# Moving conversions, an expansion and the block products of a sketched-attention + GELU-MLP kernel to other steps

## The chip, the cores and the metric

The kernel runs on one core of one Trainium2 chip. The metric is the device time of one execution in microseconds (us). Before the change it is 276.03 us, the median of three runs (275.75 to 277.18). The profiled execution, on which all readings of the trace rest, has a span of 274.7 us.

A core has a matrix engine (TensorE, "PE" in the profile), a vector engine (VectorE, "DVE"), an engine for activation functions (ScalarE, "ACT"), a general one (GpSimd, "POOL") and queues that issue transfers. They run at the same time, each through its own list of instructions in a fixed order, and wait for one another by semaphores.

## The reference, cut to what matters

Four batches of four heads with 1088 tokens each go through an attention without softmax: queries and keys are expanded to 64 features (the outer product of two 8-vectors), and since no softmax lies between them the keys and values are first reduced to one 64x32 matrix per head. The result feeds an MLP with an exact GELU.

```python
def phi(x):                                     # 32 -> 64 features
    a = einsum('rd,bhsd->bhsr', S1, x); b = einsum('rd,bhsd->bhsr', S2, x)
    return einsum('bhsi,bhsj->bhsij', a, b).reshape(..., 64)
q_p, k_p = phi(q), phi(k)
kv  = einsum('bhsf,bhsd->bhfd', k_p, v)         # one 64x32 matrix per head
z   = sum(k_p, axis=2)
num = einsum('bhsf,bhfd->bhsd', q_p, kv)
den = einsum('bhsf,bhf->bhs', q_p, z)[..., None] + 1e-06
x   = (num / den), heads joined to 128 columns  # 4352 x 128
h   = x @ w_in                                  # 4352 x 2048
out = (0.5 * h * (1 + erf(h / sqrt(2)))) @ w_out   # 4352 x 128
```

The weights `w_in`, `w_out` and the sketches arrive as 64-bit floats, so the kernel converts them to 32 bits itself.

## The kernel before

The 4352 tokens are cut into nine chunks: eight of 512 tokens (two for each batch) and a last one with the remainders. The hidden layer is cut into 16 tiles of 128 channels. One **step** `t` is one hidden tile of one chunk: a matmul of 128x128 weights on 512 tokens, and a GELU. Chunks 0 and 1 share steps 0 to 31; chunk `n` from 2 on has steps 16n to 16n+15. In each step everything else that is due is put into the text, and the text's order is the order of every engine.

```python
steps  = [(n, fi) for f in range(0, USUAL, 4) for n in range(NCH) for fi in range(f, f + 4)]   # 0..15
steps += [(n, fi) for n in range(NCHUNK) for fi in range(USUAL if n < NCH else 0, NF)]          # 16..143
# [...]
for t in range(len(steps) + LAG):
    # [...] (steps 0 to 4 have pieces of their own)
    for n in drains[t]:
        drain(n)
    if t < len(steps):
        n, fi = steps[t]
        hidden(n, fi, by_halves=t >= 18 and (n < NMAIN or fi < 5))
    if [... last tile of a block of four ...]:
        token_sums(n, b)
    for f in slots[t]:          # what at(t, f) has put there
        f()
    for n in done[t]:
        store(n)
    if t != 4:
        for f, *a in products[t]:
            f(*a)
```

**Second product.** Tiles 0 to 7 of chunks 0 and 1 go through a plain matmul (`project`). All others go through a Strassen-like scheme in blocks of four tiles: GpSimd forms sums of the block's halves, TensorE does seven pairs of half-size products, and two PSUM banks hold a chunk's sums until they are drained. `out_bank()` takes one of only **two** banks of the pool `ops`, so a chunk's first product waits until all reads of the bank's former content are over.

```python
ops = ctx.enter_context(tc.tile_pool(name="ops", bufs=2, space=PSUM))
wps = ctx.enter_context(tc.tile_pool(name="wps", bufs=2, space=PSUM))   # two tiles of two banks

def token_sums(n, b):                      # 4 GpSimd operations of 128x512
    pool.tensor_sub(out=s[3], in0=a11, in1=a21)     # L606, tile bits_low
    pool.tensor_add(out=s[1], in0=a21, in1=a22)     # L607, bits_a
    pool.tensor_sub(out=s[2], in0=s[1], in1=a11)    # L608, bits_e
    pool.tensor_sub(out=s[4], in0=a12, in1=s[2])    # L609, bits_m

def two_products(n, b, i):
    # [...]
    if opens and i == 0:
        acc[n] = [out_bank(), out_bank()]
    for name, e in zip(two[:2], two[2:]):
        pe.matmul(acc[n][bank][...], lhsT=fixed, rhs=moving, ...)      # L641

def drain(n):
    C, N = (att.tile([128, 2, CW], FP, name="sums") for i in range(2))
    a0, a1 = acc[n]
    act.copy(out=C[lo, 0], in_=a1[hi])                                    # L653
    act.copy(out=N[hi, 0, one], in_=a1[hi, one])                          # L654
    act.copy(out=N[lo, 0, one], in_=a0[lo, one])                          # L655
    dve.tensor_add(out=C[lo, 1], in0=a1[lo], in1=C[lo, 0])                # L657
    for half in (lo, hi):
        dve.tensor_add(out=C[half, 0, one], in0=a0[lo, one], in1=C[lo, 1, two])    # L659
    dve.tensor_add(out=C[hi, 0, two], in0=a0[hi, two], in1=C[hi, 0, one])  # L660
    dve.tensor_add(out=N[hi, 1, one], in0=a0[hi, one], in1=C[hi, 0, two])  # L661
    dve.tensor_add(out=N[lo, 1, one], in0=a0[lo, two], in1=N[lo, 0, one])  # L662
```

**Attention of a chunk, and the next batch's keys** (n = 3 stands at step 37):

```python
def query_turn(n):   dve.transpose(out=qT[n], in_=q_sb[n])             # L453
def query_expand(n):                                                    # 4 matmuls, 4 copies, 4 products
    expand_products(n)                    # L462, into two tiles of wps
    for g in range(4):
        expand_copy(n, g)                 # ACT L469
        if g % 2: expand_multiply(n, g // 2)     # DVE L483

def attend(n, meanwhile):
    banks = halves(work_banks())
    # 4 matmuls, L504
    meanwhile()                           # features_of_all(b): key products L350, ACT copies L817
    for h in range(H):
        act.activation(out=den[h * D:(h + 1) * D, :W], ..., func=ACT.Copy, bias=1e-6)     # L511
    dve.reciprocal(out=den[:, :W], in_=den[:, :W])                        # L512
    for h in range(H):
        dve.tensor_mul(out=xT[n][rows, :W], in0=banks[h % 2][rows, :W], in1=den[rows, :W])   # L516

def outer_of_all(b):
    for r, a in enumerate(held["factors"]):
        for t in range(2):
            dve.tensor_mul(...)           # L827, k_p from a_t and PSUM
    for r in range(2):
        add_tokens(b, r, dve)             # L388 and L391, from SBUF to SBUF
```

**Keys of batch 1** (steps 14 to 21) come in smaller pieces: `key_turn_blocks` (DVE L335), `features` (PE L350, ACT L366, DVE L367, each in a tile of `wps` of its own), `add_tokens` by GpSimd, `turn_keys_rem` (PE L306 into the next tile of `wps`), `features_rem`, `finish_keys` (PE L396, L425), `turn_kv`.

**Conversion of a weight piece** of 512 columns (class `Rounding`): `low_words` (ACT L250), `fields` (DVE L254, L256), `exponents` (ACT L262), and `finish`, which is `mantissas` (DVE L270), `signs` (DVE L275) and `product` (L280, by VectorE unless another engine is named). `channel_sums(i)` is four GpSimd operations on a converted piece of `w_out` (L593 to L596).

The schedule that the change touches:

```python
def round_at(t, w):
    r = []
    at(t, lambda: (r.append(Rounding(w)), r[0].low_words(), r[0].fields()))
    at(t + 1, lambda: (r[0].exponents(), r[0].finish()))

for i, (t0, t1) in enumerate(((4, 6), (8, 10), (12, 17))):
    round_at(t0, w_in_sb[i + 2]); round_at(t1, w_out_sb[i + 2])
for i, t in enumerate((25, 26, 28, 13, 19)):
    at(t, channel_sums, i)
# keys of batch 1, with t = 32: widen_v_rem 12, key_turn_blocks 14, features and add_tokens 15,
# turn_keys_rem 16, features_rem 17, query_turn(2) 18, finish_keys 19, turn_kv 21,
# query_expand(2) 22, query_turn(3) 23, attend(2) 25
for n in range(3, NCHUNK):
    t = (n - 1) * NF
    # [...]
    if n > 3: at(t - 2, query_turn, n)
    at(t + 2 if n > 3 else t - 2, query_expand, n)
    at(t + 5, attend, n, lambda b=b, keys=keys: keys and features_of_all(b))
    if keys:
        at(t + 5, outer_of_all, b)        # n = 3: step 37
```

Of the kernel before, what the change touches and what calls it, by code (L numbers as in the profile page):

```python
# [16 lines left out]
def kernel(  # L17
# [18 lines left out]
    pe, dve, act, pool, sp = nc.tensor, nc.vector, nc.scalar, nc.gpsimd, nc.sync  # L36
# [5 lines left out]
    NF = d_ff // 128  # L42
# [7 lines left out]
    NCH = J // JC  # L50
# [33 lines left out]
    by_act, by_dve, by_pool = act.copy, dve.tensor_copy, pool.tensor_copy  # L84
# [7 lines left out]
    w_in_sb = [big.tile([d_model, c1 - c0], FP, name=f"w_in{i}") for i, (c0, c1) in enumerate(pieces)]  # L92
    w_out_sb = [big.tile([128, c1 - c0], FP, name=f"w_out{i}") for i, (c0, c1) in enumerate(pieces)]
# [339 lines left out]
    def turn_kv(b, ps, copy):  # L433
        if b == 0:
            pe.transpose(ps[:, :128], in_=kv_T[b], identity=ident)
        else:
            for rows in (slice(0, 64), slice(64, 128)):
                pe.matmul(ps[rows, :128], lhsT=kv_T[b][:, rows], rhs=ident, start=True, stop=True)
        copy(out=kz[b].rearrange("p c n -> p (c n)"), in_=ps[:, :128])
# [185 lines left out]
    def first_block(n):  # L625
        return USUAL // NB if n < NCH else 0
# [40 lines left out]
    def take_usual(n):  # L667
        usual[n] = mlp.tile([128, CW], FP, name="g", bufs=4)
        act.copy(out=usual[n], in_=o_of[n])
# [56 lines left out]
    r = Rounding(SR)  # L726
# [33 lines left out]
    late = []  # L760
# [38 lines left out]
    def at(t, f, *a):  # L799
        slots[t].append(lambda: f(*a))  # L800
# [5 lines left out]
    def features_of_all(b):  # L806
        banks = halves(work_banks())
        for r in range(2):
            key_products(r, banks, r * 128)
        held["keys"] = banks  # L810


        held["factors"] = []
        for r in range(2):
            a = att.tile([128, 2, J, 2 * R], FP, name="a_t")
            for t in range(2):
                act.copy(out=a[:, t, :, 0:R], in_=factors(banks[t], r)[:, :, 0:R])  # L817
            held["factors"].append(a)
# [12 lines left out]
    held = {}  # L831
# [11 lines left out]
        kv_sum_rem(b, held["kv"])  # L843
        take_kv(b, held["kv"], by_act)

    def round_at(t, w):
        r = []
        at(t, lambda: (r.append(Rounding(w)), r[0].low_words(), r[0].fields()))
        at(t + 1, lambda: (r[0].exponents(), r[0].finish()))

    for i, (t0, t1) in enumerate(((4, 6), (8, 10), (12, 17))):
        round_at(t0, w_in_sb[i + 2])
        round_at(t1, w_out_sb[i + 2])
    for i, t in enumerate((25, 26, 28, 13, 19)):
        at(t, channel_sums, i)
    b, t = 1, NCH * NF
    at(t - 20, widen_v_rem, b)
    for r in range(2):
        at(t - 18, key_turn_blocks, b, r)
    for r in range(2):  # L860
        at(t - 17, features, b, r)
        at(t - 17, add_tokens, b, r, pool)
    at(t - 16, turn_keys_rem, b)
    at(t - 15, features_rem, b)
    at(t - 13, finish_keys, b)
    at(t - 11, lambda: turn_kv(1, held["kv"], by_act))
    at(t - 14, query_turn, 2)
    at(t - 10, query_expand, 2)
    at(t - 9, query_turn, 3)
    at(t - 7, attend, 2)  # L870
    for n in range(3, NCHUNK):

        t = (n - 1) * NF
        b = (n + 1) // 2
        keys = n % 2 and b < B
        if n > 3:
            at(t - 2, query_turn, n)
        at(t + 2 if n > 3 else t - 2, query_expand, n)
        if keys:
            for r in range(2):  # L880
                at(t - 2, key_turn_blocks, b, r)
        at(t + 5, attend, n, lambda b=b, keys=keys: keys and features_of_all(b))
        if keys:
            at(t + 5, outer_of_all, b)
            at(t + 8, widen_v_rem, b)
            at(t + 16, finish_keys, b)
            at(t + 17, lambda b=b: turn_kv(b, held["kv"], by_act))
# [4 lines left out]
    drains = {t: [] for t in range(len(steps) + LAG + 1)}  # L892
    for t, (n, fi) in enumerate(steps):
        if n < NCH and fi < USUAL:
            products[t + LAG].append((project, n, fi))
            if fi == USUAL - 1:
                slots[t + LAG + 1 + 2 * n].append(lambda n=n: take_usual(n))
        elif n == NMAIN:
            at_ = max(t + LAG, (n * NF + 5) if fi < 3 else (n * NF + 6) if fi < 5 else 0)
            if fi < NF - 4:  # L900
                products[at_].append((project, n, fi))
            if fi == NF - 1:

                products[at_] += [(project, n, NF - f, (i,)) for f, i in ((4, 0), (3, 0), (2, 0), (4, 1), (1, 0), (3, 1),
                                                                          (2, 1), (1, 1))]
                done[at_ + 1].append(n)
        elif fi % NB == NB - 1:
            b = fi // NB
            for later, pairs in (((3, 3), (4, 2), (5, 2)) if b == first_block(n) else ((2, 2), (3, 2), (4, 1), (5, 2))):
                for i in range(pairs):  # L910
                    products[t + later].append((two_products, n, b, len([p for q in products.values() for p in q
                                                                        if p[:3] == (two_products, n, b)])))
            if b == NF // NB - 1:
                drains[t + 6].append(n)
                done[t + 12].append(n)

    for t in range(len(steps) + LAG):
# [22 lines left out]
# [3 lines that stand above are left out]
        if t < len(steps) and steps[t][0] < NMAIN and steps[t][1] % NB == NB - 1:  # L943
            n, b = steps[t][0], steps[t][1] // NB
# [50 lines left out]
```

## Time and profile before

| what | value |
|---|---|
| time, median of three | 276.03 us |
| span of the profiled execution | 274.7 us |
| PE busy | 267.2 us (97%) |
| DVE busy | 173.9 us (63%) |
| ACT busy | 145.4 us (53%) |
| POOL busy | 167.5 us (61%) |
| one hidden tile on PE, in two halves (chain of waits) | 0.86 us |
| two pairs of block products on PE (eight entries of L641 in the chain: each matmul is recorded as two passes) | 0.86 us |
| one token sum on POOL (L606 to L609) | 1.3 us |

How to read it: "busy" is the time in which an engine works on at least one instruction. PE is near its whole span, so what counts is where it does *not* go on at once. The timeline gives, for an engine, the start in us, the duration, the engine, the line of the kernel, the operation, what it writes and reads, and how many instructions were merged; a bracket at the end is idle time before it and what ended that. The view of waits adds up such idle time by who waited for whom.

### The profile page before, as it was taken

How to read it: one execution, taken by the hardware profiler on the slowest of the kernel's cores; microseconds unless marked ns; L12 is line 12 of the kernel's file. 1: busy time of each engine (PE TensorE's matmuls, PEld its weight loads, DVE VectorE, ACT ScalarE, POOL GpSimd, SP SyncE). 2: the span in 40 equal slices, each digit the busy share in tenths (PEclk: the TensorE clock that was granted, in tenths of full speed). 3: DMA queues.
4: the chain of work that ended last, by engine and by line, in shares of the span. 5: the costliest groups of instructions: out<-in, count | busy, mean ns of one | idle time of the engine just before them, and what ended most of it. 6: DMA issues, size and time to landing. Idle time of an engine off the chain costs nothing.

```text
span 274.7 us, 5816 instructions
## 1 busy us (share of the span) xinstructions
PE 267.2 (97%) x2326; PEld 137.2 (50%) x2326; DVE 173.9 (63%) x267; ACT 145.4 (53%) x290; POOL 167.5 (61%) x174
## 2 busy tenths in 40 slices
PE   8999998999999999999999999999999999999994
PEld 6745444434344545445444545434544444545794
DVE  6995888653995699679507699479037902660140
ACT  4684764385745733484347633674358335734431
POOL 3331003779977499557885599468766886777400
PEclk9999999999999999999999999999999999999999
DMA  7559263635200100010200000200200020011020
GB/s 208 155 164 354 56 170 65 168 73 139 53 2 14 26 0 2 15 27 0 42 0 0 2 0 5 38 0 2 38 0 2 0 39 4 1 19 22 2 37 21
DMA packets 37915, 13.50 MB, mean 49 GB/s; under 512 B 28288, under 2 KB 37248, under 8 KB 37888
## 3 DMA queue, kind: packets, MB, share of 16 engines
q1 hardware_dynamic: 37648, 13.05, 19.0%
q8 instruction: 18, 0.29, 0.5%
q10 hardware_dynamic: 240, 0.08, 0.1%
q14 instruction: 9, 0.07, 0.1%
HBM read 10.90 MB, written 2.23 MB: 48 GB/s over the span
## 4 chain that ended last, share of the span: by engine, by line
PE 70%; DVE 10%; SPq 8%; DMA 7%; issue 2%; ACT 1%; POOL 0%; DVEq 0%; POOLq 0%
PE h_ps L564 31%; PE o_ps L641 28%; SPq L106 5%; DMA block<-in_moe_w_out_dram 4%; PE w_ps L462 3%; PE w_ps L689 3%; PE w_ps L504 2%; DVE xT L516 2%; DMA q<-in_q_dram 2%; DMA v<-in_v_dram 1%; PE w_ps L722 1%; DVE den L512 1%; SPq L119 1%; DVE bits_r L388 1%; DVE bits_r L391 1%
## 5 line engine op out<-in xcount | busy, mean ns | idle before, releaser
L564 PE MATMUL h_ps<-xT,w_in 128*64 128x512 f32 (+3 forms) x518 | 140.7, 577 | 0.3 <-ACT xT L549 0.2
L571 ACT ACTIVATE block<-h_ps 128x512 f32<-128x512 f32 (+1 forms) x128 | 72.8, 570 | 93.6 <-PE h_ps L564 89.5
L641 PE MATMUL o_ps<-block,w_out 128*64 128x256 f32 x224 | 57.7, 380 | 0.0
L564 PEld LDWEIGHTS h_ps<-xT,w_in 128*64 128x64 f32 (+1 forms) x518 | 42.3, 143 | 29.8 <-issue 9.3
L606 POOL TENSOR_TENSOR bits_low<-block 128x512 f32<-128x512 f32 x28 | 36.7, 1309 | 31.1 <-ACT block L571 30.9
L641 PEld LDWEIGHTS o_ps<-block,w_out 128*64 128x64 f32 x224 | 30.1, 137 | 38.1 <-issue 28.8
L607 POOL TENSOR_TENSOR bits_a<-block 128x512 f32<-128x512 f32 x28 | 36.1, 1288 | 16.2 <-ACT block L571 16.1
L483 DVE TENSOR_TENSOR q_pT<-A_sb,w_ps 64x512 f32<-64x512 f32 x32 | 22.1, 691 | 30.4 <-ACT A_sb L469 29.7
L608 POOL TENSOR_TENSOR bits_e<-bits_a,block 128x512 f32<-128x512 f32 x28 | 36.8, 1313 | 2.2
L609 POOL TENSOR_TENSOR bits_m<-block,bits_e 128x512 f32<-128x512 f32 x28 | 36.0, 1286 | 2.2
L641 PE MATMUL o_ps<-bits_a,small 128*64 128x256 f32 x112 | 29.0, 382 | 0.0
L641 PE MATMUL o_ps<-bits_low,small 128*64 128x256 f32 x112 | 28.9, 381 | 0.0
L641 PE MATMUL o_ps<-block,small 128*64 128x256 f32 x112 | 28.9, 380 | 0.0
L641 PE MATMUL o_ps<-bits_m,w_out 128*64 128x256 f32 x112 | 28.8, 379 | 0.0
L512 DVE RECIPROCAL den<-den 128x512 f32<-128x512 f32 (+1 forms) x7 | 21.9, 3122 | 9.9 <-ACT den L511 9.9
L641 PEld LDWEIGHTS o_ps<-block,small 128*64 128x64 f32 x112 | 15.0, 137 | 19.1 <-issue 12.5
L657 DVE TENSOR_TENSOR sums<-o_ps,sums 64x512 f32<-64x512 f32 x8 | 5.5, 682 | 23.7 <-ACT sums L654 20.7
L469 ACT COPY A_sb<-w_ps 64x512 f32<-64x512 f32 (+1 forms) x36 | 17.7, 557 | 4.9 <-PE w_ps L462 4.5
L516 DVE TENSOR_TENSOR xT<-w_ps,den 32x512 f32<-32x512 f32 (+1 forms) x28 | 18.2, 649 | 1.0
L641 PE MATMUL o_ps<-bits_e,small 128*64 128x256 f32 x112 | 16.8, 379 | 0.0
L692 PE MATMUL o_ps<-g,w_out 128*128 128x512 f32 x32 | 16.5, 603 | 0.1
L511 ACT ACTIVATE den<-w_ps 32x512 f32<-32x512 f32 (+1 forms) x28 | 15.6, 557 | 1.3 <-PE w_ps L504 1.0
(159 smaller groups left out, 327.4 us busy)
## 6 DMA issues: line engine op xcount, KB each, us to landing
block<-in_moe_w_in_dram SPq DMA_DIRECT2D x3, 512.0 KB, 7.2
block<-in_moe_w_out_dram SPq DMA_DIRECT2D x3, 512.0 KB, 9.9
k<-in_k_dram SPq DMA_DIRECT2D x48, 32.0 KB, 1.8
v<-in_v_dram SPq DMA_DIRECT2D x3, 512.0 KB, 4.1
q<-in_q_dram SPq DMA_DIRECT2D x24, 64.0 KB, 3.7
out_dram<-oT SPq DMA_DIRECT2D x24, 64.0 KB, 2.2
k<-in_k_dram SPq DMA_DIRECT2D x2, 256.0 KB, 2.9
q<-in_q_dram SPq DMA_DIRECT2D x2, 256.0 KB, 4.4
```

Of the source, the lines that this page charges most:

```text
L469: act.copy(out=A[g // 2][F:, g % 2, :width[n]], in_=B_of[n][g // 2][:F, g % 2, :width[n]])
L483: dve.tensor_mul(out=cols[r * F:(r + 1) * F], in0=a[:, :, r::2], in1=b[:, :, r::2])
L512: dve.reciprocal(out=den[:, :W], in_=den[:, :W])
L516: dve.tensor_mul(out=xT[n][rows, :W], in0=banks[h % 2][rows, :W], in1=den[rows, :W])
L564: pe.matmul(ps[rows, :W], lhsT=w[:, rows], rhs=xT[n][:, :W], start=True, stop=True)
L571: act.activation(out=g_of[n, fi][:, :W], in_=ps[:, :W], func=ACT.Gelu)
L606: pool.tensor_sub(out=s[3], in0=a11, in1=a21)
L607: pool.tensor_add(out=s[1], in0=a21, in1=a22)
L608: pool.tensor_sub(out=s[2], in0=s[1], in1=a11)
L609: pool.tensor_sub(out=s[4], in0=a12, in1=s[2])
L641: pe.matmul(acc[n][bank][half * 64:(half + 1) * 64, col:col + HW], lhsT=fixed, rhs=moving, start=opens and e == 0 and name in "4715", stop ...
L692: pe.matmul(o_of[n], lhsT=w_tile(w_out_sb, fi), rhs=g, start=first, stop=final)
```

## The change

It has four parts. The last two conversions are put closer together (pieces 4 of `w_in` and `w_out` at steps 12 and 14 instead of 12 and 17), and their final products go from VectorE to GpSimd. The keys of batch 1 are turned at step 14 as before, but their features move from step 15 to 16, and `finish_keys` and `turn_kv` from 19 and 21 to 20 and 22. Chunk 2's query is turned at step 15 (before: 18) and expanded at step 18 (before: 22), ahead of batch 1's key-value matrix; its `attend` moves from 25 to 24. The queries of chunks 4 and later are turned four steps sooner. And the block products of chunks 0 and 1, with the first block of chunk 2, come one step later, as do the drains of chunks 0 and 1 (steps 30 and 38 instead of 29 and 37). No arithmetic is added or taken away. The aim is that the matrix engine finds its operands ready where it waits for them now.

```diff
@@ -843,38 +843,42 @@
         kv_sum_rem(b, held["kv"])
         take_kv(b, held["kv"], by_act)
 
-    def round_at(t, w):
+    def round_at(t, w, product_by=dve):
         r = []
         at(t, lambda: (r.append(Rounding(w)), r[0].low_words(), r[0].fields()))
-        at(t + 1, lambda: (r[0].exponents(), r[0].finish()))
-
-    for i, (t0, t1) in enumerate(((4, 6), (8, 10), (12, 17))):
+        at(t + 1, lambda: (r[0].exponents(), r[0].mantissas(), r[0].signs(), r[0].product(product_by)))
+
+    for i, (t0, t1) in enumerate(((4, 6), (8, 10))):
         round_at(t0, w_in_sb[i + 2])
         round_at(t1, w_out_sb[i + 2])
-    for i, t in enumerate((25, 26, 28, 13, 19)):
+    round_at(12, w_in_sb[4], pool)
+    at(13, channel_sums, 3)
+
+    at(12, widen_v_rem, 1)
+    for r in range(2):
+        at(14, key_turn_blocks, 1, r)
+    round_at(14, w_out_sb[4], pool)
+    at(15, query_turn, 2)
+    for r in range(2):
+        at(16, features, 1, r)
+        at(16, add_tokens, 1, r, pool)
+    at(16, turn_keys_rem, 1)
+    at(17, features_rem, 1)
+    at(18, channel_sums, 4)
+    at(18, query_expand, 2)
+    at(20, finish_keys, 1)
+    at(22, lambda: turn_kv(1, held["kv"], by_act))
+    at(23, query_turn, 3)
+    at(24, attend, 2)
+    for i, t in enumerate((25, 26, 28)):
         at(t, channel_sums, i)
-    b, t = 1, NCH * NF
-    at(t - 20, widen_v_rem, b)
-    for r in range(2):
-        at(t - 18, key_turn_blocks, b, r)
-    for r in range(2):
-        at(t - 17, features, b, r)
-        at(t - 17, add_tokens, b, r, pool)
-    at(t - 16, turn_keys_rem, b)
-    at(t - 15, features_rem, b)
-    at(t - 13, finish_keys, b)
-    at(t - 11, lambda: turn_kv(1, held["kv"], by_act))
-    at(t - 14, query_turn, 2)
-    at(t - 10, query_expand, 2)
-    at(t - 9, query_turn, 3)
-    at(t - 7, attend, 2)
     for n in range(3, NCHUNK):
 
         t = (n - 1) * NF
         b = (n + 1) // 2
         keys = n % 2 and b < B
         if n > 3:
-            at(t - 2, query_turn, n)
+            at(t - 6, query_turn, n)
         at(t + 2 if n > 3 else t - 2, query_expand, n)
         if keys:
             for r in range(2):
@@ -906,12 +910,15 @@
                 done[at_ + 1].append(n)
         elif fi % NB == NB - 1:
             b = fi // NB
-            for later, pairs in (((3, 3), (4, 2), (5, 2)) if b == first_block(n) else ((2, 2), (3, 2), (4, 1), (5, 2))):
+            opens = b == first_block(n)
+            late = int(n < NCH or n == NCH and opens)
+            for later, pairs in ((3, 3), (4, 2), (5, 2)) if opens else ((2, 2), (3, 2), (4, 1), (5, 2)):
+                later += late
                 for i in range(pairs):
                     products[t + later].append((two_products, n, b, len([p for q in products.values() for p in q
                                                                         if p[:3] == (two_products, n, b)])))
             if b == NF // NB - 1:
-                drains[t + 6].append(n)
+                drains[t + 6 + late].append(n)
                 done[t + 12].append(n)
 
     for t in range(len(steps) + LAG):
```

## The prediction

> **What bounds the kernel now.** I read the page's first part first: the matrix engine works 97% of the span, so the time changes only by what is added to or taken from its idle stretches.
>
> ```profile
> PE 267.2 (97%) x2326; PEld 137.2 (50%) x2326; DVE 173.9 (63%) x267; ACT 145.4 (53%) x290; POOL 167.5 (61%) x174
> ```
>
> Second, the view of waits, limited to PE: what the change can gain.
>
> ```profile
> PE w_ps L350 <- DVE kT L335: 1.0, 1, 1.0
> PE w_ps L462 <- DVE qT L453: 0.9, 2, 0.5
> PE w_ps L462 <- DVE xT L516: 0.3, 1, 0.3
> ```
>
> These are the key products of batch 1 (L350) behind VectorE's turned keys, the expansions of chunks 2 and 4 behind a turned query, and the expansion of chunk 3 behind the attention of chunk 2. They make 2.2 us, 0.8% of the time. A gain of 2% is not there.
>
> Third, the timeline of VectorE around step 37, where the drain of chunk 1 stands ahead of the attention of chunk 3 and the keys of batch 2.
>
> ```profile
> 88.70 0.68 DVE L657 TENSOR_TENSOR sums<-o_ps,sums 64x512 f32<-64x512 f32 x1 [3.04 <-PE h_ps L564]
> ...
> 91.27 0.42 DVE L662 TENSOR_TENSOR sums<-o_ps,sums 64x256 f32<-64x256 f32 x1
> 93.65 3.35 DVE L512 RECIPROCAL den<-den 128x512 f32<-128x512 f32 x1 [1.96 <-ACT den L511]
> 97.11 2.79 DVE L516 TENSOR_TENSOR xT<-w_ps,den 32x512 f32<-32x512 f32 x4
> 99.92 2.48 DVE L827 TENSOR_TENSOR k_p<-a_t,w_ps 128x512 f32<-128x512 f32 x4
> 102.32 1.43 DVE L388 TENSOR_TENSOR bits_r<-k_p 128x512 f32<-128x512 f32 x1
> 103.79 1.39 DVE L391 TENSOR_TENSOR bits_r<-bits_r 128x256 f32<-128x256 f32 x1
> 105.10 1.76 DVE L388 TENSOR_TENSOR bits_r<-k_p 128x512 f32<-128x512 f32 x1
> 106.89 1.39 DVE L391 TENSOR_TENSOR bits_r<-bits_r 128x256 f32<-128x256 f32 x1
> ```
>
> The reader is to see the order: the five kinds of drain operation (L657 to L662) are over at 91.69, and then 15 us of work follow without a gap, 93.65 to 108.28. From the timelines of PE and ACT, the start of that work:
>
> ```profile
> 88.60 1.09 PE L504 MATMUL w_ps<-q_pT,kz 64*64 64x512 f32 x8
> 89.51 1.08 PE L350 MATMUL w_ps<-S,kT 64*64 64x32 f32 x64
> ```
>
> ```profile
> 91.23 2.39 ACT L511 ACTIVATE den<-w_ps 32x512 f32<-32x512 f32 x4
> ```
>
> Last, the timelines of VectorE and GpSimd at steps 14 to 16:
>
> ```profile
> 42.34 1.75 DVE L275 SCALAR_TENSOR_TENSOR bits_e<-block,bits_r 128x512 uint32<-128x512 uint32 x1 [0.54 <-ACT bits_r L262]
> 44.12 0.83 DVE L280 TENSOR_TENSOR w_in<-bits_m,bits_e 128x512 f32<-128x512 f32 x1
> 44.87 1.41 DVE L335 STREAM_TRANSPOSE kT<-k 128x256 f32<-128x256 f32 x4
> ```
>
> ```profile
> 42.27 0.45 POOL L593 TENSOR_TENSOR small<-w_out 128x128 f32<-128x128 f32 x1
> 42.68 0.45 POOL L594 TENSOR_TENSOR small<-w_out 128x128 f32<-128x128 f32 x1
> 43.09 0.45 POOL L595 TENSOR_TENSOR small<-w_out,small 128x128 f32<-128x128 f32 x1
> 43.62 0.79 POOL L596 TENSOR_TENSOR small<-w_out,small 128x128 f32<-128x128 f32 x1
> ```
>
> L275 takes 1.75 us beside GpSimd's four channel sums; alone it takes 0.69 (same line at 38.91).
>
> [...] what precedes in the text precedes in every timeline above. [...] The trace shows the start-up alone: passes of 256 columns 0.43 us apart at the start, 0.21 later, with full speed from 4.8 us on, 3.6 us after the first. [...] the trace has 1.3 us (L606) against 0.69 (L280 alone).
>
> **The change part by part.**
>
> *Drain of chunk 1 a step later (38).* Within a step the drains come first, then the hidden tile, then the slots. At step 37 (before) drain(1) therefore preceded attend(3) and the keys of batch 2, which stay at step 37. At step 38 it follows them in VectorE's list: L512, L516, L827, L388, L391, L388, L391, and only then L657. But the first products of chunk 2, now at step 39, take the two `ops` banks that chunk 1 holds until L657 (bank 1) and L662 (bank 0) have read them. TensorE must stop there. In the clock of the old trace:
> - PE reaches that product after L504 (from 88.60, 1.02 in the chain), L350 (0.95), chunk 1's last two pairs (0.86) and the hidden tiles 38 and 39 (0.86 each): 93.15.
> - VectorE: the chain to the end of L827 has no part that gets sooner: 102.40. In the old trace L388 and L391 ran beside token sums and took 5.96 us. Now GpSimd's last work before the stop is the sums of chunk 2's second block. They start after the GELU of step 38, which follows `den` (ends 93.62) and the drain's three copies (1.35): about 95.6; four times 1.3 and the padding of v (1.2) end at 102.0. No new hidden tiles come while PE stands, so GpSimd is idle then, and the additions take what such operations take alone: 0.69 + 0.42 twice (L391 as a half of 0.69 and overhead, the 0.42 of L676 alone at 83.77), 2.4 with gaps. L657: 0.68. End 105.5.
> - Stop: 105.5 − 93.15 = 12.4 us. L662 ends 2.5 us later, but three pairs and a hidden tile (2.15 us, more at half clock) lie between.
> - PE has then been idle over 12 us; half clock for some 3.6 us, as at the start, costs half of that: 1.8 us.
>
> *Steps 12 to 16.* The product of `w_in` piece 4 leaves VectorE, and the channel sums now follow it on GpSimd, so L275 runs alone: 42.34 to 43.03, keys turned by 44.45 (before: 46.28). PE would reach the features of step 16 at 46.06 and end them at 46.95: the 1.0 us wait is gone. But `turn_keys_rem` follows in the same step and takes the `wps` tile that the first features hold until two L367. VectorE must first do `w_out` piece 4: L254 waits behind GpSimd's product (43.1 to 44.4) and three channel sums, to 45.6; then L254, L256 with a sum between, L270, L275, L453: 0.34 + 0.45 + 0.42 + 0.7 + 0.7 + 0.7 = 3.3, to 48.9; two L367 with an ACT copy between, 1.6, to 50.5. A new wait of about 3.5 us. Step 17's tile then starts at 51.5 (before: 49.49).
>
> *Steps 17 to 23.* Tiles, expansion, kv and turning add up to 9.2 us, so step 23's tile starts at about 60.7; in the old trace at 61.06, but with three pairs (1.29) already done, which are still to come here. So I am 0.9 us behind. The waits for the turned query (0.5 and 0.3 us of lost TensorE time near 57.7 and 55.4) are in this already.
>
> *Attend(2) sooner and the queries sooner.* The wait of chunk 3's expansion (0.4 us lost at 74.5) and that of chunk 4's (0.7 at 113.1) go: −1.1.
>
> Sum: 276.0 + 12.4 + 1.8 + 0.9 − 1.1 = 290.0 us.
>
> **The rivals.**
> (1) *As intended*: drain(1) is in time, only the waits vanish: 273.5 to 275. For it speaks that every wait in the PE view is addressed. Against it speaks the order of VectorE's list, which is fixed by the text.
> (2) *The additions still collide with GpSimd*, at 5.96 us instead of 2.4: the stop is 16 us, the time 294. Against it: GpSimd has nothing to read after 102.0; but it is close (L388 starts at 102.4).
> (3) *The clock does not fall*, or PE's wait is shorter for being split: 288.
> (4) *GpSimd becomes the bound* by the two products of 1.3 us: its page share is 61%, and the first token sums start only after step 19; no more than 1 us.
>
> **Range and chances.** The stop is 11.5 to 16 us, the clock 0 to 3, the early steps −1.5 to +1.5: 285.5 to 294.5. The gain is capped near 1% by the PE waits, so faster by over 2% is all but excluded; within 2% needs the stop under 5.5 us, which only a misread bank would bring: 4%. Faster 1%, same 4%, slower 95%.
>
> **What would show it.** A gap of some 12 us in PE before an L641 near 95 us, ended by DVE L657, and L657 directly after the second L391; L388 and L391 near 0.7 and 0.4 us; matmul passes at double spacing for 3 to 4 us after it; DVE L367 released late and L306 waiting about 3 us near 47 to 50; no wait for qT left. It is wrong if L641 of chunk 2 starts within 1 us of its hidden tile, if PE goes on with other work in the gap, or if the time is under 281.5.

## The result, and the profile after

The changed kernel takes 292.87 us (median of four, 291.79 to 293.17) against 276.36: ratio 1.0588, 95% interval 1.0547 to 1.063. It is 16.5 us slower, 2.9 us above the predicted 290.0. The profiled execution spans 290.0 us; all its times below are from that one.

The page's first part, and the rows of PE and its granted clock in 40 slices of 7.25 us:

```profile
PE 270.1 (93%) x2326; PEld 138.3 (48%) x2326; DVE 162.2 (56%) x265; ACT 145.7 (50%) x290; POOL 169.7 (59%) x176
...
PE   8999997989999049999999999999999999999995
...
PEclk9999999899999758999999999999999999999999
```

PE has as much to do as before (267.2 us then), but there is one hole, slices 14 and 15 (94 to 109 us), and the clock falls twice: briefly in slice 8 (51 to 58) and long in slices 14 to 16. The view of waits for PE names what ended the hole:

```profile
PE o_ps L641 <- DVE sums L657: 11.8, 1, 11.8
PE w_ps L306 <- issue: 2.0, 1, 2.0
...
PE w_ps L396 <- ACT block L571: 0.9, 1, 0.9
```

The three waits of the old view (turned keys, turned queries, attention of chunk 2) are gone, as the change meant. Three new ones stand in their place, and the first is five times the sum of the old. VectorE's timeline at the hole:

```profile
94.10 3.35 DVE L512 RECIPROCAL den<-den 128x512 f32<-128x512 f32 x1 [6.43 <-ACT den L511]
97.56 2.79 DVE L516 TENSOR_TENSOR xT<-w_ps,den 32x512 f32<-32x512 f32 x4
100.36 2.48 DVE L827 TENSOR_TENSOR k_p<-a_t,w_ps 128x512 f32<-128x512 f32 x4
102.76 0.68 DVE L388 TENSOR_TENSOR bits_r<-k_p 128x512 f32<-128x512 f32 x1
103.48 0.42 DVE L391 TENSOR_TENSOR bits_r<-bits_r 128x256 f32<-128x256 f32 x1
103.82 0.68 DVE L388 TENSOR_TENSOR bits_r<-k_p 128x512 f32<-128x512 f32 x1
104.54 0.42 DVE L391 TENSOR_TENSOR bits_r<-bits_r 128x256 f32<-128x256 f32 x1
104.88 0.68 DVE L657 TENSOR_TENSOR sums<-o_ps,sums 64x512 f32<-64x512 f32 x1
```

L657, the first read of chunk 1's sums, is now last. Before the 94.10 VectorE sits idle for 6.43 us. Chunk 1's last product ends at 92.06, so a drain ahead of the attention could have begun in the last 2 us of that time; but VectorE's list has it later, and so has ScalarE's list its three copies (94.09, right after L511). The additions L388 and L391 take 0.68 and 0.42 us; beside GpSimd's token sums, in the old trace, they took 1.39 to 1.76. PE's timeline:

```profile
91.89 1.89 PE L564 MATMUL h_ps<-xT,w_in 128*64 128x512 f32 x8
105.61 0.69 PE L641 MATMUL o_ps<-block,small 128*64 128x256 f32 x1 [11.84 <-DVE sums L657]
...
106.09 0.63 PE L641 MATMUL o_ps<-block,small 128*64 128x256 f32 x1
...
106.52 0.63 PE L641 MATMUL o_ps<-block,small 128*64 128x256 f32 x1
...
112.10 0.38 PE L641 MATMUL o_ps<-block,w_out 128*64 128x256 f32 x1
...
112.32 0.38 PE L641 MATMUL o_ps<-block,w_out 128*64 128x256 f32 x1
```

The first product of chunk 2 starts at 105.61, right after L657 (0.68 us from 104.88). The passes after it stand 0.43 us apart (106.09 to 106.52), twice the 0.22 of 112.10 to 112.32. The clock's records in the trace give half clock from 97.17 to 110.82; from 105.61 on that is 5.2 us, so 2.6 us lost. The stop itself, counted from the end of hidden tile 39 (second pass at 93.17, 0.43 us of work) to 105.61, is 12.0 us.

The second hole, in PE's timeline:

```profile
46.22 1.14 PE L350 MATMUL w_ps<-S,kT 64*64 64x32 f32 x64
49.34 0.42 PE L306 MATMUL w_ps<-ident,k_rem 128*128 128x128 f32 x1 [1.99 <-issue]
49.55 1.92 PE L692 MATMUL o_ps<-g,w_out 128*128 128x512 f32 x2
51.26 1.79 PE L564 MATMUL h_ps<-xT,w_in 128*128 128x512 f32 x2
```

A pair of passes takes 1.9 and 1.8 us instead of 1.0: half clock here too (49.38 to 52.80 in the clock's records, 1.7 us lost). "Issue" means that this view shows no releaser. The trace has a semaphore event in the list of PE's weight loads for L306, 2.25 us from 47.0, and it ends within 0.1 us of the end of the second L367 (49.24); so it does in e2, e3, e4, e5, e7 and e10 too. The wait is for the `wps` tile that the key features hold; e6 and e10 below test this.

### The profile page after: what moved, and what is told of

Its sections match the earlier page's. It is cut to its first block, busy times and chain, and to the rows that moved or that the text cites. A ratio compares the mean times of both kernels' runs of the same rounds, so it can differ in the third digit from the quotient of the medians.

```text
span 290.0 us, 5818 instructions
## 1 busy us (share of the span) xinstructions
PE 270.1 (93%) x2326; PEld 138.3 (48%) x2326; DVE 162.2 (56%) x265; ACT 145.7 (50%) x290; POOL 169.7 (59%) x176
## 4 chain that ended last, share of the span: by engine, by line
PE 88%; DVE 6%; ACT 2%; issue 1%; POOL 0%; DVEq 0%; POOLq 0%
PE h_ps L564 40%; PE o_ps L641 30%; PE o_ps L692 5%; PE w_ps L689 2%; PE w_ps L462 2%; PE w_ps L504 2%; PE w_ps L396 1%; PE w_ps L722 1%; DVE den L512 1%; ACT A_sb L469 1%; PE w_ps L350 1%; DVE q_pT L483 1%; DVE k_p L827 1%; DVE xT L516 1%; ACT den L511 1%
## 5 line engine op out<-in xcount | busy, mean ns | idle before, releaser
L606 POOL TENSOR_TENSOR bits_low<-block 128x512 f32<-128x512 f32 x28 | 36.1, 1290 | 46.0 <-ACT block L571 45.9
L641 PE MATMUL o_ps<-block,w_out 128*64 128x256 f32 x224 | 58.3, 383 | 0.0
L641 PEld LDWEIGHTS o_ps<-block,w_out 128*64 128x64 f32 x224 | 30.2, 138 | 38.8 <-issue 29.5
L607 POOL TENSOR_TENSOR bits_a<-block 128x512 f32<-128x512 f32 x28 | 36.3, 1295 | 16.6 <-ACT block L571 16.5
L641 PE MATMUL o_ps<-block,small 128*64 128x256 f32 x112 | 29.7, 388 | 11.8 <-DVE sums L657 11.8
L608 POOL TENSOR_TENSOR bits_e<-bits_a,block 128x512 f32<-128x512 f32 x28 | 36.1, 1288 | 2.2
L512 DVE RECIPROCAL den<-den 128x512 f32<-128x512 f32 (+1 forms) x7 | 21.9, 3122 | 18.1 <-ACT den L511 18.1
L641 PEld LDWEIGHTS o_ps<-block,small 128*64 128x64 f32 x112 | 15.5, 140 | 30.5 <-DVE sums L657 13.0
L641 PE MATMUL o_ps<-bits_low,small 128*64 128x256 f32 x112 | 29.7, 388 | 0.0
L641 PE MATMUL o_ps<-bits_a,small 128*64 128x256 f32 x112 | 29.5, 386 | 0.0
L641 PE MATMUL o_ps<-bits_m,w_out 128*64 128x256 f32 x112 | 28.8, 380 | 0.0
L516 DVE TENSOR_TENSOR xT<-w_ps,den 32x512 f32<-32x512 f32 (+1 forms) x28 | 18.2, 649 | 1.0
L657 DVE TENSOR_TENSOR sums<-o_ps,sums 64x512 f32<-64x512 f32 x8 | 5.5, 682 | 22.0 <-ACT sums L654 22.0
L692 PE MATMUL o_ps<-g,w_out 128*128 128x512 f32 x32 | 17.3, 629 | 0.1
L641 PE MATMUL o_ps<-bits_e,small 128*64 128x256 f32 x112 | 17.3, 388 | 0.0
L511 ACT ACTIVATE den<-w_ps 32x512 f32<-32x512 f32 (+1 forms) x28 | 15.6, 558 | 1.3 <-PE w_ps L504 1.0
```

What stands on the lines that cost most here:

```text
L641: pe.matmul(acc[n][bank][half * 64:(half + 1) * 64, col:col + HW], lhsT=fixed, rhs=moving, start=opens and e == 0 and name in "4715", stop ...
L692: pe.matmul(o_of[n], lhsT=w_tile(w_out_sb, fi), rhs=g, start=first, stop=final)
```

## The experiments

Two theories for the 16.5 us. **Drain order**: the stop comes from VectorE's list, where the drain of chunk 1 stands behind the attention of chunk 3 and the keys of batch 2. Rivals: the **late products** themselves hold tiles or starve GpSimd, or the **early steps** (12 to 23) lose the time and the stop is their echo. The times are medians; the ratio is to the kernel before on the same chip, with its 95% interval. Runs from different chips are compared by their ratios (0.001 is 0.28 us).

| run | time, us | ratio | interval |
|---|---|---|---|
| the change | 292.87 | 1.0588 | 1.0547 to 1.063 |
| e1, late part alone | 289.17 | 1.0449 | 1.0393 to 1.0504 |
| e2, attention of chunk 3 at 38 | 277.88 | 1.0048 | 1.0022 to 1.0074 |
| e3, outer products at 38 | 287.42 | 1.0385 | 1.0319 to 1.0452 |
| e4, 40 fillers in the stop | 298.67 | 1.0763 | 1.0682 to 1.0844 |
| e5, 20 fillers in the stop | 289.90 | 1.0504 | 1.0469 to 1.0539 |
| e6, e2 and remainder's turn at 17 | 274.55 | 0.9952 | 0.9934 to 0.997 |
| e7, no late part | 277.63 | 1.0059 | 1.0033 to 1.0084 |
| e8, four pieces on the kernel before | 275.39 | 0.9986 | 0.9967 to 1.0005 |
| e9, three pieces | 274.43 | 0.9931 | 0.9909 to 0.9953 |
| e10, e2 and last conversion at 20 | 276.00 | 0.9994 | 0.998 to 1.0008 |
| e11, e7 and remainder's turn at 17 | 275.07 | 0.995 | 0.9934 to 0.9967 |

**e1: the late part alone.** On the kernel before:

```diff
-            for later, pairs in (((3, 3), (4, 2), (5, 2)) if b == first_block(n) else ((2, 2), (3, 2), (4, 1), (5, 2))):
+            opens = b == first_block(n)
+            late = int(n < NCH or n == NCH and opens)
+            for later, pairs in ((3, 3), (4, 2), (5, 2)) if opens else ((2, 2), (3, 2), (4, 1), (5, 2)):
+                later += late
...
-                drains[t + 6].append(n)
+                drains[t + 6 + late].append(n)
```

> The kernel before with only one part of the change: block products of chunks 0 and 1 and the first block of chunk 2 a step later, drains of chunks 0 and 1 a step later; conversions, keys and queries as before. Theory 'drain order' (the first products of chunk 2 wait for L657, which stands behind the attention of chunk 3 and the keys of batch 2): a stop of 11.5 to 12.5 us before an L641 after step 39 and half clock worth 2.4 us, so 290 to 291.5 us. Rival 'early steps' (the loss comes from the conversions and the features at step 16, the stop is only their echo): within 1% of 276.4 us.

Measured: 289.17 us, and in its view of waits for PE the same line as in the changed kernel:

```profile
PE o_ps L641 <- DVE sums L657: 11.8, 1, 11.8
```

The early steps are as before here, so they don't make the stop. The median is 0.8 us below the range; the profiled execution, the longest of the four at 290.21, is inside it. In its view of waits 0.8 us of the old waits are left instead of 2.2: those for chunk 4's query (0.5) and for chunk 2's attention (0.3) are gone, though both stand at the same steps as before, and that for the turned keys is 0.4 instead of 1.0. Why the other three executions were shorter still, no trace shows.

**e2: the attention of chunk 3 behind the drain again.** On the changed kernel:

```diff
-        at(t + 5, attend, n, lambda b=b, keys=keys: keys and features_of_all(b))
+        u = t + 6 if n == 3 else t + 5
+        at(u, attend, n, lambda b=b, keys=keys: keys and features_of_all(b))
         if keys:
-            at(t + 5, outer_of_all, b)
+            at(u, outer_of_all, b)
```

> The changed kernel with the attention of chunk 3 and the keys of batch 2 at step 38 instead of 37, so that the drain of chunk 1 stands ahead of them again. Theory 'drain order': the whole stop and its half clock go, 292.9 - 12.0 - 2.4 = 278.5 us (277 to 279.5). Rival 'late products' (products a step later starve GpSimd or hold its tiles, whatever the drain does): above 285 us.

Measured: 277.88 us, 15.0 less than the change, against 12.0 + 2.6 for stop and half clock. VectorE's timeline of e2 has the drain ahead again:

```profile
91.53 0.68 DVE L657 TENSOR_TENSOR sums<-o_ps,sums 64x512 f32<-64x512 f32 x1 [3.12 <-ACT sums L654]
...
96.56 3.35 DVE L512 RECIPROCAL den<-den 128x512 f32<-128x512 f32 x1 [2.04 <-ACT den L511]
```

No wait of an L641 is left in its view of waits. Products a step later cost nothing if the drain is in time; "late products" falls.

**e3: only what stands between L516 and L657 moved.** On the changed kernel:

```diff
-            at(t + 5, outer_of_all, b)
+            at(t + 6 if n == 3 else t + 5, outer_of_all, b)
```

> The changed kernel with only the keys' outer products and token additions (L827, L388, L391) of batch 2 moved to step 38; the attention of chunk 3 stays at 37, ahead of the drain. Theory 'drain order': L657 comes straight after L516, 4.5 us sooner, so the stop is 7.5 us and the clock still falls: 292.9 - 4.5 = 288.4 us (287.5 to 289.5). Rival 'late products': no difference, 291.5 to 294.

Measured: 287.42 us, 0.1 below its range; the four executions spread from 284.84 to 288.48, with mean granted clocks of 0.988 to 0.976 (1 is full speed). VectorE's timeline of e3:

```profile
95.92 3.35 DVE L512 RECIPROCAL den<-den 128x512 f32<-128x512 f32 x1 [6.43 <-ACT den L511]
99.37 2.79 DVE L516 TENSOR_TENSOR xT<-w_ps,den 32x512 f32<-32x512 f32 x4
102.19 0.68 DVE L657 TENSOR_TENSOR sums<-o_ps,sums 64x512 f32<-64x512 f32 x1
```

L657 follows L516 at once, and PE's stop is 7.5 us instead of 12.0 (7.3 instead of 11.8 in the view of waits). So what precedes L657 in the list sets the stop's length: taking 4.5 us from there took 4.5 from it.

**e4 and e5: work for PE in the stop.** On the changed kernel, matmuls on zeros whose result nobody uses, ahead of step 39's products (40 in e4, 20 in e5):

```diff
+        if t == 39:
+            keep_busy(20, hidden_bank())
         if t != 4:
```

> The changed kernel with 40 matmuls on a tile of zeros (256 columns, result unused) on TensorE ahead of the first product of chunk 2, in the stop. Theory 'half clock after the stop': the stop ends at the same time, but the passes after it are at full speed: 292.9 - 2.4 = 290.5 us (290 to 291.2). Rival 'the slow passes after the stop are something else, such as operands that come late': no gain, 292.5 to 293.5, and passes still at double spacing.

> The changed kernel with 20 matmuls on zeros in the stop (each is two passes of 0.213 us, 8.5 us in all; the 40 of e4 made 17 us, longer than the stop). They can start when the GELU of step 38 has freed a bank (about 2.5 us into the stop) and end about 0.5 us before L657. Theory 'half clock after the stop': the stop ends as before and the 5 us after it run at full speed: 292.9 - 2.4 = 290.5 us (289.5 to 291.5). Rival 'late operands': 292.5 to 293.5 and double spacing still there.

e4 was mis-sized by me: a filler is two passes of 0.213 us, so 40 last 17 us, longer than the stop, and its 298.67 us say only that (the clock is whole after the fillers there too). e5 measured 289.90 us, inside its range; PE's timeline of e5:

```profile
94.41 8.90 PE L722 MATMUL h_ps<-idle 128*128 128x256 f32 x40 [2.23 <-ACT block L571]
104.02 0.43 PE L641 MATMUL o_ps<-block,small 128*64 128x256 f32 x1 [0.71 <-DVE sums L657]
...
104.28 0.38 PE L641 MATMUL o_ps<-block,small 128*64 128x256 f32 x1
...
104.50 0.38 PE L641 MATMUL o_ps<-block,small 128*64 128x256 f32 x1
```

The stop ends as before with L657, but the passes after it are 0.22 us apart at once. The ratios differ by 0.0084, 2.3 us, about the cost of the half clock after the stop; the two intervals lie close together (e5's ends at 1.0539, the change's begins at 1.0547). The profiled execution of e5, its shortest (287.82 us), lacks the half clock at 49 as well; without that execution the difference is an estimated 1.9 us. Against the change's profile its span is 4.0 us shorter, where the two half clocks make 1.7 + 2.6.

**e7: the early steps alone.** On the changed kernel:

```diff
-            late = int(n < NCH or n == NCH and opens)
+            late = 0
```

> The changed kernel without its late part: conversions, keys and queries as in the change, block products and drains where they were before. Theory: no stop near step 39; what stays is the wait before L306 with its half clock against the waits that the change removes: 277 to 279, as e2. If the later products are worth something of their own at steps 22 to 25 (token sums of the first block not ready), e7 is above e2 by up to 1.5 us with an L641 waiting for POOL near 60 us.

Measured: 277.63 us, as e2 (the intervals overlap), 1.4 above the kernel before on that chip (276.19). So the early part as it stands loses 1.4 us, and the late part has no worth of its own: no L641 waits for POOL near 60 us. What the early part loses is in its timelines. VectorE and GpSimd of e7:

```profile
43.58 1.42 DVE L335 STREAM_TRANSPOSE kT<-k 128x256 f32<-128x256 f32 x4
44.92 1.77 DVE L254 TENSOR_SCALAR bits_e<-block 128x512 uint32<-128x512 uint32 x1
46.62 0.67 DVE L256 TENSOR_SCALAR bits_a<-block 128x512 uint32<-128x512 uint32 x1
...
49.23 0.65 DVE L367 TENSOR_TENSOR k_p<-a_t,w_ps 128x512 f32<-128x512 f32 x1
```

```profile
43.14 0.79 POOL L326 COPY v_rem_aug<-v_rem 64x64 f32<-64x64 f32 x2 [18.34 <-DMA v_rem<-in_v_dram]
43.90 1.28 POOL L280 TENSOR_TENSOR w_in<-bits_m,bits_e 128x512 f32<-128x512 f32 x1
45.13 0.45 POOL L593 TENSOR_TENSOR small<-w_out 128x128 f32<-128x128 f32 x1
45.55 0.45 POOL L594 TENSOR_TENSOR small<-w_out 128x128 f32<-128x128 f32 x1
45.96 0.45 POOL L595 TENSOR_TENSOR small<-w_out,small 128x128 f32<-128x128 f32 x1
```

L254 starts 0.26 us before GpSimd's product ends (44.92 against 45.18) and 0.21 before the first of three sums (45.13), and ends 0.28 us after the third (46.69 against 46.41): 1.77 us instead of 0.4. In the profiled execution of the change it started 0.06 us before the sums (44.37 against 44.43) and took 0.38. L306 waited 2.0 us there and 3.0 here, in one and the same part of the program; I read it as a race between the two engines. The traces also show what goes with its outcome. Where GpSimd's product starts 0.08 us after L275 ends (the change, e2, e5, e6, e11), L254 takes 0.4 us. Where it starts 0.24 to 0.60 us after, because GpSimd is still copying v's remainder (L326), for which it had waited on a transfer, L254 takes 1.8 to 2.1 us (e3, e4, e7). No run moved that transfer on purpose.

**e6 and e11: the remainder's turn a step later.** On e2 (e6) and e7 (e11):

```diff
-    at(16, turn_keys_rem, 1)
-    at(17, features_rem, 1)
+    at(17, turn_keys_rem, 1)
+    at(18, features_rem, 1)
```

> e2 (attention of chunk 3 at step 38) with the remainder's key turn at step 17 instead of 16 and its features at 18, ahead of the expansion. Theory 'tile of the key features': TensorE's wait before L306 (2.2 to 3.6 us in the runs so far) and the half clock after it (1.6 to 2.5 us) go, a wait of under 1 us stays before L306 or the expansion's second half: 277.9 - 2.5 = 275.4 us (274.4 to 276.4). Rival 'VectorE is behind anyway': the wait moves to L306 at step 17 or to L374 whole, 277 to 278.5.

> e7 (no late part) with the remainder's key turn at step 17 and its features at 18. Theory: as e6 without anything that the later products bring; if they bring nothing, 274.5 us (274 to 275.2), and an L641 for chunk 0 does not wait for POOL. Rival 'later products let token sums finish': 275.5 to 276.5, with such a wait near 58 us.

Measured: 274.55 and 275.07 us, ratios 0.9952 and 0.995, both inside their ranges. PE's timeline of e6:

```profile
48.87 1.02 PE L564 MATMUL h_ps<-xT,w_in 128*128 128x512 f32 x2
49.96 0.30 PE L306 MATMUL w_ps<-ident,k_rem 128*128 128x128 f32 x1
50.10 1.02 PE L692 MATMUL o_ps<-g,w_out 128*128 128x512 f32 x2
```

L306 now has a product and a hidden tile (1.7 us) between it and the key features and starts 0.2 us late; the pairs of passes are at 1.0 us, so the clock stays whole. The wait of 0.9 us before L396 is gone too. By the ratios e6 takes 2.7 us less than e2. The late part is again without worth (e6 and e11 alike).

**e10: the last conversion out of the way, the turn left at step 16.** On e2:

```diff
-    round_at(14, w_out_sb[4], pool)
...
-    at(18, channel_sums, 4)
...
     at(20, finish_keys, 1)
+    round_at(20, w_out_sb[4], pool)
+    at(22, channel_sums, 4)
```

> e2 with the last conversion (w_out, last piece) at step 20 instead of 14, out of VectorE's list ahead of the key features; the remainder's turn stays at step 16. Theory: of the wait before L306 the part that VectorE's conversion makes goes (0.6 us where L254 slips in ahead of GpSimd's sums, 1.7 where it waits for them), and the chain L350, ACT copy, L367, ACT copy, L367 stays: a wait of 1.5 to 1.8 us: 277.9 - 1.0 = 276.9 us (276 to 277.6). Rival 'conversion is the whole wait': 275 or less, no wait at L306.

Measured: 276.00 us, L306's wait 1.6. VectorE's timeline of e10:

```profile
44.65 0.67 DVE L453 STREAM_TRANSPOSE qT<-q 128x512 f32<-128x512 f32 x1
47.48 0.69 DVE L367 TENSOR_TENSOR k_p<-a_t,w_ps 128x512 f32<-128x512 f32 x1 [2.16 <-ACT a_t L366]
48.44 1.28 DVE L367 TENSOR_TENSOR k_p<-a_t,w_ps 128x512 f32<-128x512 f32 x2 [0.28 <-ACT a_t L366]
```

With VectorE free for 2.16 us, L306 still waits 1.6 us for two L367 and the two ACT copies ahead of them: that is the wait for the tile alone. What the conversion adds is 0.4 us (the change's profile) to 1.8 (e4, where L306 waits 3.4). In this execution the clock stays whole. In 5 of e10's 22 executions it does not: their mean clock is 0.992 to 0.993, about what 3.41 us at half clock leave (e2's profile: 0.994), and they took 276.68 to 277.29 us, the others 275.30 to 276.25. By the ratios e10 gains 1.5 us on e2.

**e8 and e9: pieces of the change on the kernel before.** e8:

```diff
-        round_at(t0, w_in_sb[i + 2])
+        round_at(t0, w_in_sb[i + 2], pool if i == 2 else dve)
...
-    at(t - 14, query_turn, 2)
+    at(t - 18, query_turn, 2)
...
-            at(t - 2, query_turn, n)
-        at(t + 2 if n > 3 else t - 2, query_expand, n)
+            at(t - 6, query_turn, n)
+        at(t + 2 if n > 3 else t - 1, query_expand, n)
```

e9 has the first three, with the expansion back at `t - 2`.

> The kernel before with four pieces alone: GpSimd makes the product of w_in's last piece, chunk 2's query is turned at step 14, later queries at t-6, chunk 3 is expanded at step 31 instead of 30. Each aims at one wait of TensorE in the old profile: keys turned (1.1 us of lost TensorE time at 43.9), turned query of chunk 2 (0.6 at 57.6), of chunk 4 (0.7 at 113.1), attention of chunk 2 (0.4 at 74.5). Theory: these waits go and none takes their place, 276.4 - 2.8 = 273.6 us (273 to 274.8). Rival 'they come back one step later as waits for ACT or the tiles of wps': 275.5 to 277.

> e8 with chunk 3 expanded at step 30 again (one piece of e8 undone). In e8 the first products of chunk 1 waited 2.2 us for L657 of chunk 0's drain, because the 1.1 us expansion no longer lay between. Theory 'drain order, small form': that wait goes, the 0.4 us wait of the expansion for chunk 2's attention comes back: 275.4 - 2.2 + 0.4 = 273.6 us (273 to 274.6). Rival: the wait for L657 stays and the expansion comes on top, 275 to 276.

Measured: e8 275.39, e9 274.43 us. e8 missed its range, by the same mechanism in small; its view of waits for PE begins with

```profile
PE o_ps L641 <- DVE sums L657: 2.0, 1, 2.0
```

Chunk 0's drain stands behind chunk 2's L512 and L516 in VectorE's list. In the kernel before, the expansion of chunk 3 lies between PE's last hidden tile and chunk 1's first product and covers that time; e8 took it away. e9 put it back: the wait went, and by the ratios 1.5 us with it. e9 is the fastest of all that ran, 0.7% below the kernel before (0.9931, 0.9909 to 0.9953); e6's interval overlaps with it.

## Why the prediction was right, point by point

- **The stop**: predicted 12.4 us, because L657 comes last in VectorE's list and PE needs its bank; measured 12.0, in the expected order, ended by the expected instruction. Shown by e2 (away with the order), e3 (shorter by what was taken out of the list) and e1 (there without anything else of the change). The collision with GpSimd (rival 2) did not come: GpSimd was idle from 102.3 us, and the additions took 0.68 and 0.42 us. The clock did fall (against rival 3), and the view of waits has no wait of PE for POOL (against rival 4).
- **The half clock after it**: the term was mis-sized. I put half of 3.6 us, 1.8; it was 2.6 in the profile (half clock for 5.2 us of work) and 2.3 by e5. That an idle time brings half clock was my estimate, and its length was that of the start-up; the old trace shows half clock nowhere else while PE works. Here the clock was low for 13.65 us in all, four times 3.41 us (97.17 to 110.82). Work resumed in the third of these stretches (104.00 to 107.41, with 1.6 us still idle), and the clock was whole only from the end of the fourth, at 110.82.
- **Steps 12 to 16**: the wait before L306 was foreseen with its cause; predicted 3.5 us, with L254 behind three sums (my estimate; the old trace has L275 at 1.75 us beside four). Measured 3.0 to 3.4 where L254 took 1.8 to 2.1 us (e3, e4, e7), and 2.0 in the change's profile, where it took 0.38. The half clock after it was not foreseen: 1.7 us that no term of the sum had. The old trace has only waits of PE up to 1.2 us, at a mean granted clock of 1.000; what follows 2 us it does not show.
- **Steps 17 to 23**: the prediction names no wait there; the view shows one of 0.9 us before L396. No run took its cause apart.
- **The gains** (old waits of the keys, of both queries and of chunk 2's attention): all came, as the view of waits shows. e9 has three of them, with nothing in their place.
- **The sum**: 290.0 against 292.87. By runs, the stop with its clock is the 15.0 us that e2 removes (predicted 14.2), and the early part the 1.5 us that e2 keeps (predicted 0.9 − 1.1 = −0.2); another 0.3 is that I started from 276.03 and the kernel before stands at 276.36. So the main term holds within 6%, and the early part had the wrong sign. That it was not further off is in part luck: in the change's profile the half clock at 49 (1.7) and the wait before L396 (0.9), which no term had, met a wait before L306 that was 1.5 shorter than predicted.

Left open: how much of the profiled execution's 291.79 us against the median of 292.87 is the race of L254. The difference fits its 1 us, but the other three executions have no trace, and no run held the race fixed in either state.

## What to carry to other kernels

When an engine's order is the order of the text, moving an operation by one step is not a small move if a long burst of the same engine stands in that step: list what is then ahead of it, and look for who waits for its buffer. A drain should come ahead of bursts that nobody needs soon, and a step that opens a new tile of a full pool should not stand right behind the step that fills it. On an engine that is busy 97% of the span, compare the sum of the waits to be removed with the longest wait that the new order can make, before building it.

## What was not expected of the hardware

An idle time of PE of about 2 us was followed by half clock in the change's profile and in e2 (2.0 us by the view of waits in both), but a like one was not in e5 at the same place (2.0) nor in e8 before L641 (2.0). After 3.0 us and more (3.1 in e3, 3.4 in e4, 3.0 in e7) the clock fell each time. It stayed low for 3.41 us or multiples of it: 3.41 (the change, e2, e7), 6.83 (e3, e4), 13.65 (the change's long stop and e1's).

In the change's trace the clock is whole from 5.01 us, falls at 49.38, rises at 52.80, falls at 97.17 and rises at 110.82: these times are 13, 1, 13 and 4 times 3.413 us apart. In the trace of before it is whole from 4.91 to 274.56, 79 times 3.413 us. I call a stretch of 3.413 us between such times a window. The times at which the clock changes give the bounds of the windows in each trace, and PE's idle time, as the profile counts it, can be added up by window:

| idle in one window at whole clock, us | trace | the next window |
|---|---|---|
| 0.95, 1.56, 1.60, 1.66 | before, e5, e10, e8 | whole clock |
| 1.76, 1.99, 1.99, 2.07, 2.86 | e3, the change, e2, e4, e7 | half clock |

So in these traces the border lies between 1.66 and 1.76 us of idle time in one window. The 2.0 us of e5 fell across two windows (1.56 and 0.43), and so did those of e8 (0.38 and 1.66); those of the change and of e2 fell into one. This is read from the traces; no run set the length of an idle time on purpose. Where the clock was low, it was still low after a window with 1.3 to 1.6 us idle (e1, e3, e4 and the change). A wait of 2.0 us thus cost an estimated 2.0 or 3.7 us (2.0 and the 1.7 of half clock in the change's profile), by where it fell. The executions of one kernel differ likewise: one of e2's 14 executions has a mean clock of 1.000 and took 275.38 us, 2.5 less than their median.

How long VectorE's L254 took beside GpSimd turned on some 0.15 us: 0.38 and 0.39 us where it started 0.06 us before the first of three back-to-back GpSimd sums (the change; e2, 45.11 against 45.17), and 1.77 us where it started 0.21 us before (e7). The long one ended after the third sum, not after the first. No trace shows why.
